# Routing attention into a squared-ReLU block, one core: the second pair's queries and keys turned by transposing transfers

## The chip, the core and the metric

The kernel runs on one core of one Trainium2 chip. The metric is the device time of one execution in microseconds (us). The core has TensorE (PE, matrix products, with its own queue of weight loads, PEld), VectorE (DVE), ScalarE (ACT), GpSimd (POOL) and SyncE (SP). Transfers (DMA) are issued from the queues of SP and ACT (SPq and ACTq in the rows) and carried by 16 DMA engines. SBUF is the working memory, PSUM holds what TensorE writes.

## The reference

Attention of 4 batches with 8 heads, 768 positions and 64 features, in which a query sees only the keys whose nearest centroid (of 16 for each head) is its own; then a block with a squared ReLU over the 3072 rows of 512.

```python
q_assign = np.argmax(np.einsum('bhsd,hcd->bhsc', q_n, c_n), axis=-1)
k_assign = np.argmax(np.einsum('bhsd,hcd->bhsc', k_n, c_n), axis=-1)
mask = q_assign[:, :, :, None] == k_assign[:, :, None, :]
scores = scale * np.matmul(q, k.transpose(0, 1, 3, 2))
scores = np.where(mask, scores, -1000000000.0)
attn = np.exp(scores - np.max(scores, axis=-1, keepdims=True))
attn = attn / (np.sum(attn, axis=-1, keepdims=True) + 1e-09)
x = np.matmul(attn, v)          # then (B,H,S,D) -> (B*S, H*D)
h = x @ w_in
out = (np.maximum(h, 0.0) ** 2) @ w_out
```

## The kernel before

**Pairs.** Attention goes in 16 pairs of heads (`for p in range(NG)`), each some 20 us long, and the second block follows. Everything here happens in the first 55 us, in pairs 0 and 1. All engines follow the order in which the code is written; nothing is scheduled behind the author's back (`manual_schedule`). A queue runs its instructions in order, so one that waits holds all behind it.

**Turned operands.** A product needs queries and keys with features along partitions (`qkT`). Pair 0 is turned by TensorE from the loaded tiles (`turn_first`, line 275), because it is wanted first. Pair 1 is also turned by TensorE (`turn`, line 289, in three parts of eight small products, each followed by a copy on ACT). From pair 2 on a transfer does it: ACT splits each float into two 16-bit words (`split_words`, line 307: four copies for a pair, two for the queries and two for the keys), a transfer stores the words in DRAM (`words`), and a transposing transfer (`turn_words`, line 323, on SP's queue) brings them back turned.

**Marks.** `logits` multiplies queries and keys by the centroids, `turn_logits` turns the result on DVE (tile `lt`), and `number` finds the largest of 16. Several equal maxima are resolved to the first by a product with `order` and a second maximum. For pair 0 the marks are a one-hot tile `oh`, turned by TensorE (`turn_onehot`) and copied out by ACT (line 410) and DVE (lines 415, 419). For later pairs `number` makes three rows of marks (`marks_t`), a small transfer stores them (`far`), and two more bring them back as the operand `rows` (line 386), one for each head of the pair.

**Tiles.** A pair has nine score tiles. Each is a `mask` product and a `score` product into one PSUM tile `sc` of three, then an exponential on ACT (line 463). A tile can begin when the exponential of the tile three places before has read its PSUM tile. Six tiles have 512 queries, three have 2 times 256. Then `times_v` multiplies the nine results by the values into PSUM `V` (shown as av_a) and `M` (av_b), `add_up` sums the weights, and the next pair follows. DVE adds up the exponentials (line 466), which `add_up` needs.

**Loads.** Pairs 0 to 2 and the first values are loaded at the start; `load_qk(3)`, three blocks of weights and the next values follow on SP's queue, `load_qk(4)` and later ones on ACT's queue. Each tile of queries, keys or values is 128 x 768 floats (0.39 MB), a block of weights 128 x 1024 (0.52 MB). A flag at the end (`check_sums`) sends the program to `general_path` if a sum in `seen` is unusable.

Of the kernel before, what the change touches and what calls it, by code (L numbers as in the profile page):

```python
# [8 lines left out]
F32 = mybir.dt.float32  # L9
# [16 lines left out]
def kernel(  # L26
# [197 lines left out]
    seen = const.tile([P, NG * NBL], F32, name="seen")  # L224
# [64 lines left out]
    def turn(pair, part, bank):  # L289
        if part == 0:  # L290
            qkT[pair] = qktp.tile([P, 2 * NCH, P], F32, name="qkT")
        for i in range(4):
            which, c = divmod(4 * part + i, NCH)
            for e in range(2):
                nc.tensor.matmul(
                    bank[D * e : D * (e + 1), P * i : P * (i + 1)],
                    lhsT=raw[pair][which][:, e, c], rhs=ident, start=True, stop=True,
                )
        nc.scalar.copy(
            out=qkT[pair][:, 4 * part : 4 * part + 4].rearrange("p c n -> p (c n)"), in_=bank  # L300
        )
        if part == 2:
            raw.pop(pair)

    words = {}

    def split_words(pair, which, queue=nc.sync):
        if pair >= NG:
            return
        if which == 0:  # L310
            words[pair] = dram.tile([2 * NCH, P, 2, 2 * D], U16, name="words")
        flat = loads.tile([P, NCH, 2, 2 * D], U16, name="flat", tag="qk")
        src = raw[pair][which].bitcast(U16).rearrange("p h c (d two) -> p h c two d", two=2)
        for e in range(2):
            nc.scalar.copy(out=flat[:, :, :, D * e : D * (e + 1)], in_=src[:, e])
        queue.dma_start(
            words[pair][NCH * which : NCH * (which + 1)].rearrange("c p two d -> p c two d"),
            flat,
        )
        if which == 1:  # L320
            raw.pop(pair)

    def turn_words(pair):
        if pair >= NG:
            return
        qkT[pair] = qktp.tile([P, 2 * NCH, P], F32, name="qkT")
        nc.sync.dma_start(
            qkT[pair].rearrange("p c n -> p (c n)").bitcast(U16),
            words.pop(pair).rearrange("c p two d -> (c p two) d"), transpose=True,
        )  # L330
# [17 lines left out]
    def number(pair):  # L348
# [8 lines left out]
        nc.vector.reduce_max(out=mx, in_=src, axis=AX.X)  # L357
        nc.vector.tensor_tensor(out=best, in0=src, in1=over_c(mx), op=ALU.is_ge)
# [4 lines left out]
        if pair == 0:  # L363
            nc.vector.tensor_tensor(
                out=oh.rearrange("p b e c -> p (b e) c")[:, :, 0:C], in0=best, in1=over_c(mx),
                op=ALU.is_equal,
            )
            return
# [21 lines left out]

    def turn_onehot():
# [5 lines left out]
        for half, bank in enumerate((sc.pop("oh")[:, 0], M)):  # L397
# [210 lines left out]

    centroids_norm()
# [5 lines left out]
    turn_first(1, 1, halves[1], nc.vector.tensor_copy)  # L615
    logits(0, begin("ls"))
    for i in ("oh", 0, 1):
        begin(i)
    turn_logits(0)
    number(0)  # L620

# [8 lines left out]
    for p in range(NG):  # L630
        if p == 0:
            load_qk(3)
            load_ahead(0)
        if p == HP + 1:
            nc.sync.dma_start(x_far[FEED[3]], xT.pop(FEED[3]))
        if p:
# [3 lines left out]
            turn_words(p + 2)  # L640
# [9 lines left out]
        if p == 0:  # L650
            for i in range(2):
                turn(1, i, (V, M)[i])
                score(p, i, 0, True)
            turn_onehot()
            for t in rows_of:
                nc.vector.memset(t, 0.0)
            turn(1, 2, V)
            for i in range(NB):
                if i == 2:
                    begin(i)  # L660
                    score(p, i, 0, True)
                mask(p, i, 0, False)
                exponential(i)
        else:
# [7 lines left out]
        if p < 2:  # L672
# [28 lines left out]
        split_words(p + 3, 1)  # L701
        load_qk(p + 4, (nc.scalar, nc.scalar))
# [969 lines left out]
    def check_sums():  # L1672
# [3 lines left out]
            out=flag[0:1], in0=every, scalar1=UP * float(P * NG * NBL), scalar2=None, op0=ALU.is_lt  # L1676
# [280 lines left out]
```

## Time and profile before

| | |
|---|---|
| median of 3 runs | 865.0 us (864.05 to 865.22) |
| the profiled execution | 863.94 us |
| its span in the profile | 862.0 us (1.94 us lie around it) |
| TensorE busy | 852.3 us, 99% of the span |
| VectorE busy | 741.0 us, 86% |
| ScalarE busy | 452.3 us, 52% |
| GpSimd busy | 242.2 us, 28% |

Times in the rows count from the start of the span. A timeline row has start, duration, engine, line, operation, output and input; in brackets stands the idle time before it and what ended that. Consecutive equal instructions are merged (x2, x3), and the duration then is that of the whole. Rows of the chain have start, duration and what the end of the program hung on at that time. The profiled execution is 1.06 us below the median.

### The profile page before, as it was taken

How to read it: one execution, taken by the hardware profiler on the slowest of the kernel's cores; microseconds unless marked ns; L12 is line 12 of the kernel's file. 1: busy time of each engine (PE TensorE's matmuls, PEld its weight loads, DVE VectorE, ACT ScalarE, POOL GpSimd, SP SyncE). 2: the span in 40 equal slices, each digit the busy share in tenths (PEclk: the TensorE clock that was granted, in tenths of full speed). 3: DMA queues.
4: the chain of work that ended last, by engine and by line, in shares of the span. 5: the costliest groups of instructions: out<-in, count | busy, mean ns of one | idle time of the engine just before them, and what ended most of it. 6: DMA issues, size and time to landing. Idle time of an engine off the chain costs nothing.

```text
span 862.0 us, 15526 instructions
## 1 busy us (share of the span) xinstructions
PE 852.3 (99%) x5883; PEld 648.9 (75%) x5883; DVE 741.0 (86%) x1189; ACT 452.3 (52%) x697; POOL 242.2 (28%) x202
## 2 busy tenths in 40 slices
PE   9999999999999999999999999999999999999997
PEld 5454444444444455557899999999999999999997
DVE  6798888888888899999779988789888898887786
ACT  5877766777775557752212692222269322693120
POOL 0000000000000046762466737130223902237000
PEclk9999999999999999999999999999999999999999
DMA  7787798677666217729895554459447895433542
GB/s 258 162 194 201 216 268 197 183 198 196 177 176 178 64 61 249 241 85 336 329 336 195 206 186 152 179 162 337 149 183 230 288 379 191 183 140 137 214 153 71
DMA packets 149443, 173.30 MB, mean 201 GB/s; under 512 B 57226, under 2 KB 126962, under 8 KB 146034
## 3 DMA queue, kind: packets, MB, share of 16 engines
q1 hardware_dynamic: 132802, 151.89, 55.8%
q10 hardware_dynamic: 16560, 20.35, 7.3%
q8 instruction: 48, 0.79, 0.4%
q14 instruction: 33, 0.27, 0.1%
HBM read 110.93 MB, written 50.27 MB: 187 GB/s over the span
## 4 chain that ended last, share of the span: by engine, by line
PE 88%; DVE 6%; DMA 2%; issue 1%; ACT 1%; POOL 1%; SPq 0%; DVEq 0%; POOLq 0%
PE bank L1365 23%; PE bank L1098 15%; PE sc L447 14%; PE av_a L481 10%; PE bank L1262 6%; PE av_b L481 5%; PE more L1098 5%; PE sc L456 4%; PE bank L811 3%; PE sc L335 1%; PE sc L500 1%; DMA wt<-w_far 1%; DVE g L1177 1%; DVE w_raw L155 1%; DVE g L767 1%
## 5 line engine op out<-in xcount | busy, mean ns | idle before, releaser
L463 ACT ACTIVATE ex<-sc 128x1024 f32<-128x1024 f32 x144 | 144.4, 1026 | 38.0 <-PE sc L447 31.9
L447 PE MATMUL sc<-qkT 64*128 64x512 f32 (+1 forms) x768 | 151.0, 484 | 0.0
L167 POOL TENSOR_TENSOR w_in<-w_in,w_raw 128x512 int32<-128x512 int32 x16 | 21.4, 1338 | 294.4 <-DVE w_in L159 278.2
L1083 POOL TENSOR_TENSOR g<-g,home 128x768 f32<-128x768 f32 x30 | 55.7, 1876 | 152.4 <-DVE home L1177 102.2
L447 PEld LDWEIGHTS sc<-qkT 64*128 64x128 f32 x768 | 67.1, 188 | 41.0 <-issue 29.8
L481 PE MATMUL av_a<-ex,v_raw 128*64 128x512 f32 x384 | 85.9, 596 | 0.0
L466 DVE TENSOR_TENSOR total<-total,ex 128x1024 f32<-128x1024 f32 x64 | 78.7, 1229 | 6.5
L1613 ACT COPY spare<-bank 128x128 f32<-128x128 f32 x35 | 9.2, 263 | 136.5 <-issue 84.8
L1365 PE MATMUL bank<-wt,l 128*128 128x128 f32 x544 | 72.0, 275 | 0.4 <-DVE l L557 0.4
L1365 PE MATMUL bank<-wt,home 128*128 128x128 f32 x552 | 70.5, 275 | 0.0
L1365 PEld LDWEIGHTS bank<-wt,l 128*128 128x128 f32 x544 | 66.2, 192 | 0.6 <-issue 0.5
L1365 PEld LDWEIGHTS bank<-wt,home 128*128 128x128 f32 x552 | 66.0, 192 | 0.0
L1177 DVE TENSOR_TENSOR g<-bank,g 128x384 f32<-128x384 f32 (+2 forms) x108 | 53.7, 506 | 13.0 <-PE bank L1098 8.4
L481 PEld LDWEIGHTS av_a<-ex,v_raw 128*64 128x64 f32 x384 | 26.2, 137 | 51.0 <-issue 50.3
L1067 ACT COPY home<-bank 128x384 f32<-128x384 f32 x66 | 30.9, 480 | 56.4 <-PE bank L1098 55.7
L456 PE MATMUL sc<-rows 64*128 64x512 bf16 (+1 forms) x360 | 60.5, 323 | 0.0
L787 ACT ACTIVATE g<-g 128x768 f32<-128x768 f32 (+1 forms) x77 | 55.7, 723 | 2.4
L786 ACT ACTIVATE g<-g 128x768 f32<-128x768 f32 (+1 forms) x77 | 54.8, 711 | 2.3 <-DVE g L1177 1.2
L481 PE MATMUL av_b<-ex,v_raw 128*64 128x256 f32 x384 | 44.2, 379 | 0.0
L456 PEld LDWEIGHTS <-rows 64*128 64x128 bf16 x360 | 18.5, 94 | 33.0 <-issue 29.2
L481 PEld LDWEIGHTS av_b<-ex,v_raw 128*64 128x64 f32 x384 | 27.6, 137 | 20.7 <-issue 5.7
L1365 PE MATMUL bank<-wt,g 128*128 128x128 f32 x304 | 38.8, 275 | 0.0
(296 smaller groups left out, 1852.5 us busy)
## 6 DMA issues: line engine op xcount, KB each, us to landing
wt<-right_far SPq DMA_DIRECT2D x11, 1792.0 KB
wt<-w_far SPq DMA_DIRECT2D x20, 896.0 KB
words<-flat SPq DMA_DIRECT2D x26, 384.0 KB
w_raw<-in_moe_w_in_dram SPq DMA_DIRECT2D x16, 512.0 KB
w_raw<-in_moe_w_out_dram SPq DMA_DIRECT2D x16, 512.0 KB
wt<-right_far SPq DMA_DIRECT2D x7, 1024.0 KB
v_raw<-in_v_dram SPq DMA_DIRECT2D x16, 384.0 KB
rb<-far_r SPq DMA_DIRECT2D x30, 192.0 KB
```

Of the source, the lines that this page charges most:

```text
L447: nc.tensor.matmul(sc[i][:, e, cols], lhsT=qkT[pair][rows, NCH + c], rhs=qkT[pair][rows, n.start // P : n.stop // P], start=first, stop=no ...
L456: nc.tensor.matmul(sc[i][:, e, cols], lhsT=ohT[pair][rows, 1, c * P : (c + 1) * P], rhs=ohT[pair][rows, 0, columns(i)], start=first, stop= ...
L463: nc.scalar.activation(out=ex[i], in_=sc.pop(i), func=ACT.Exp, scale=SCALE)
L466: eng.tensor_tensor(out=out, in0=a, in1=b, op=ALU.add)
L481: nc.tensor.matmul(bank[D * e : D * (e + 1), 0 : n.stop - n.start], lhsT=raw_v[pair][:, e, c], rhs=ex[i][:, e, cols], start=c == 0, stop=c ...
L786: nc.scalar.activation(out=to, in_=to, func=ACT.Relu)
L787: nc.scalar.square(to, to)
L1083: nc.gpsimd.tensor_tensor(out=of_four(to, s)[:, :, half], in0=of_four(base, s)[:, :, half], in1=beside[s].rearrange("p u m n -> p (u m) n" ...
L1098: nc.tensor.matmul(bank[:, QT * u : QT * (u + 1)], lhsT=lefts[j, s](u)[i], rhs=operand[i], start=begins and u == 0, stop=True, skip_group_ ...
L1177: nc.vector.tensor_tensor(out=out, in0=one, in1=two, op=ALU.add)
L1262: nc.tensor.matmul(bank, lhsT=left[j][:, f], rhs=right(j)[:, f], start=begins and f == 0, stop=True, skip_group_check=True,)
L1365: nc.tensor.matmul(bank, lhsT=left[:, f], rhs=rhs[:, f], start=(f == 0), stop=(f == F4 - 1))
```

## The change

Pair 1 is no longer turned by TensorE: `turn` is gone. Its words are split by ACT before pair 0's marks are copied out, stored from ACT's queue, and brought back by two transposing transfers (queries, keys) that stand on SP's queue ahead of `load_qk(3)`, the weights and the next values. The split words lie in spare tiles of the exponentials' pool.

Pair 0's marks are one comparison with the maximum, without `order`, the second maximum and the comparison with it. `count_marks` adds up the ones of each partition and writes 0.5 into one more column of `seen` where they are exactly 24 (one for each row of queries and keys), and 0 where they are not, which sends the program to the general path.

The last copy of pair 0's turned keys is cut in two, half on ACT, half on DVE; the DVE half waits for the ACT half. `logits(1)` and what follows move from behind tile 2 of pair 0 to behind its second tile of 256, and write to `M`. Pair 1 writes three scores first and then the three masks; `split_words(3, 1)`, `turn_words(3)` and `load_qk(4)` move from pair 0 into pair 1, behind its third exponential. From pair 2 on nothing changes.

```diff
@@ marks of the first pair, in number()
         nc.vector.reduce_max(out=mx, in_=src, axis=AX.X)
+        if pair == 0:
+            nc.vector.tensor_tensor(
+                out=oh.rearrange("p b e c -> p (b e) c")[:, :, 0:C], in0=src, in1=over_c(mx),
+                op=ALU.is_ge,
+            )
+            return
         nc.vector.tensor_tensor(out=best, in0=src, in1=over_c(mx), op=ALU.is_ge)
...
         nc.vector.reduce_max(out=mx, in_=best, axis=AX.X)
-        if pair == 0:
...
-            return
+    def count_marks():
+        marked = small.tile([P, 1], F32, name="marked")
+        nc.vector.reduce_sum(
+            out=marked, in_=oh.rearrange("p b e c -> p (b e) c")[:, :, 0:C], axis=AX.XY
+        )
+        nc.vector.tensor_scalar(
+            out=seen[:, NG * NBL :], in0=marked, scalar1=2.0 * NBL, scalar2=0.5,
+            op0=ALU.is_equal, op1=ALU.mult,
+        )
@@ turn_words
-        nc.sync.dma_start(
-            qkT[pair].rearrange("p c n -> p (c n)").bitcast(U16),
-            words.pop(pair).rearrange("c p two d -> (c p two) d"), transpose=True,
-        )
+        far = words.pop(pair)
+        for i in range(0, 2 * NCH, NCH if pair == 1 else 2 * NCH):
+            c = slice(i, i + (NCH if pair == 1 else 2 * NCH))
+            nc.sync.dma_start(
+                qkT[pair][:, c].rearrange("p c n -> p (c n)").bitcast(U16),
+                far[c].rearrange("c p two d -> (c p two) d"), transpose=True,
+            )
@@ ahead of the loop
+    def by_two(out, in_):
+        nc.scalar.copy(out=out[:, 0:QT], in_=in_[:, 0:QT])
+        nc.vector.tensor_copy(out=out[:, QT:], in_=in_[:, QT:])
...
-    turn_first(1, 1, halves[1], nc.vector.tensor_copy)
+    turn_first(1, 1, halves[1], by_two)
...
     number(0)
+    for i in range(2):
+        split_words(1, i, nc.scalar)
@@ in the loop
         if p == 0:
+            turn_words(1)
             load_qk(3)
...
         if p == 0:
             for i in range(2):
-                turn(1, i, (V, M)[i])
                 score(p, i, 0, True)
             turn_onehot()
+            count_marks()
             for t in rows_of:
                 nc.vector.memset(t, 0.0)
-            turn(1, 2, V)
+            begin(2)
+            score(p, 2, 0, True)
             for i in range(NB):
-                if i == 2:
-                    begin(i)
-                    score(p, i, 0, True)
                 mask(p, i, 0, False)
                 exponential(i)
+        elif p == 1:
+            for i in range(NB):
+                begin(i)
+                score(p, i, 0, True)
+            for i in range(NB):
+                mask(p, i, 0, False)
+                exponential(i)
+            split_words(3, 1)
+            turn_words(3)
+            load_qk(4, (nc.scalar, nc.scalar))
...
         for i in range(NCH, NCH + NB):
             tile_of(p, i)
+            if p == 0 and i == NCH + 1:
+                sc["ls"] = M.rearrange("p (a n) -> p a n", a=1)
+                logits(1, sc["ls"])
+                turn_logits(1)
+                number(1)
...
         if p == 0:
             split_words(3, 0)
-        split_words(p + 3, 1)
-        load_qk(p + 4, (nc.scalar, nc.scalar))
+        else:
+            split_words(p + 3, 1)
+            load_qk(p + 4, (nc.scalar, nc.scalar))
```

Lines behind the edits shift: line 315 of before is 305 of the change, 327 is 320, 335 is 328, 383 is 376, 386 is 379, 410 is 413, 447 is 450, 456 is 459, 463 is 466.

SP's queue of before, from the first values to the first sums (`w_raw` weights, `far` and `rows` the marks of pair 1, `qkT<-words` the turning of pair 2, then the words of pair 3):

```order
L105 DMA v_raw<-in_v_dram 128x2x384
L95 DMA q_raw<-in_q_dram 128x2x384
L95 DMA k_raw<-in_k_dram 128x2x384
L128 DMA w_raw<-in_moe_w_in_dram 128x1024 x3
L105 DMA v_raw<-in_v_dram 128x2x384
L383 DMA far<-marks_t 128x3x32
L386 DMA rows_168<-far 3x4x384 x2
L327 DMA_TRANSPOSE qkT<-words 128x3072
L316 DMA words<-flat 128x6x256 x2
L515 DMA far_r<-seen 128x12
```

The same stretch of SP's queue with the change:

```order
L105 DMA v_raw<-in_v_dram 128x2x384
L320 DMA_TRANSPOSE qkT<-words 128x1536 x2
L95 DMA q_raw<-in_q_dram 128x2x384
L95 DMA k_raw<-in_k_dram 128x2x384
L128 DMA w_raw<-in_moe_w_in_dram 128x1024 x3
L105 DMA v_raw<-in_v_dram 128x2x384
L320 DMA_TRANSPOSE qkT<-words 128x3072
L376 DMA far<-marks_t 128x3x32
L379 DMA rows_168<-far 3x4x384 x2
L306 DMA words<-flat 128x6x256
L518 DMA far_r<-seen 128x12
```

Two transposing transfers for pair 1 now stand ahead of the six loads, and the marks of pair 1 (`far`, `rows`) have moved from ahead of pair 2's transposing transfer to behind it.

ACT of before at the head of pair 0 (`av_a`, `av_b` and `sc` are PSUM tiles, the `ex` of line 410 is the turned one-hot tile):

```order
L285 COPY qkT<-sc 128x384
L299 COPY qkT<-av_a 128x512
L299 COPY qkT<-av_b 128x512
L410 ACTIVATE ex<-sc 128x6x2x32 x2
L299 COPY qkT<-av_a 128x512
L463 ACTIVATE ex<-sc 128x1024 x6
L315 COPY flat<-q_raw 128x12x64 x2
```

The same place with the change:

```order
L285 COPY qkT<-sc 128x384
L613 COPY qkT<-sc 128x192
L305 COPY ex<-q_raw 128x12x64 x2
L306 DMA words<-ex 128x6x256
L305 COPY ex<-k_raw 128x12x64 x2
L306 DMA words<-ex 128x6x256
L413 ACTIVATE ex<-av_a 128x6x2x32 x2
L466 ACTIVATE ex<-sc 128x1024 x6
```

The three copies of line 299 are gone; four splitting copies, two issues of transfers and half a copy stand ahead of the copies of the marks.

ACT of before in pair 1 (from the last copy of pair 0's result on; here `flat<-q_raw` and `flat<-k_raw` are pair 4's split, the loads are pair 5's):

```order
L490 COPY xT<-av_b 128x256
L463 ACTIVATE ex<-sc 128x1024 x6
L315 COPY flat<-q_raw 128x12x64 x2
L463 ACTIVATE ex<-sc 128x1024 x3
L315 COPY flat<-k_raw 128x12x64 x2
L95 DMA q_raw<-in_q_dram 128x2x384
L95 DMA k_raw<-in_k_dram 128x2x384
```

The same place with the change:

```order
L493 COPY xT<-av_b 128x256
L466 ACTIVATE ex<-sc 128x1024 x3
L305 COPY flat<-k_raw 128x12x64 x2
L95 DMA q_raw<-in_q_dram 128x2x384
L95 DMA k_raw<-in_k_dram 128x2x384
L466 ACTIVATE ex<-sc 128x1024 x3
L305 COPY flat<-q_raw 128x12x64 x2
L466 ACTIVATE ex<-sc 128x1024 x3
```

Two splitting copies of pair 3 and the issue of pair 4's loads now stand between the third and the fourth exponential of pair 1.

## Rows read from the trace of the kernel before

**Rows 1.** The page: granted clock in 40 slices, and the chain's shares.
```profile
PEclk9999999999999999999999999999999999999999
...
PE 88%; DVE 6%; DMA 2%; issue 1%; ACT 1%; POOL 1%; SPq 0%; DVEq 0%; POOLq 0%
```

**Rows 2.** The chain in order of time, 0 to 70 us (start, us, what).
```profile
9.39 1.02 PE av_a L295 x16
10.42 1.06 PE sc L447 x4
...
13.56 0.44 PE sc L402 x6
...
17.89 0.39 PE sc L456 x2
18.28 0.86 PE sc L447 x4
...
24.55 5.30 PE av_a L481 x24
...
32.44 0.78 PE sc L500 x8
...
53.35 0.32 PE sc L456
```

**Rows 3.** The timeline, ACT and its queue, 14 to 34 us.
```profile
14.04 0.87 ACT L410 ACTIVATE ex<-sc 128x384 bf16<-128x384 bf16 x2 [0.90 <-PE sc L402]
...
15.89 2.86 ACT L463 ACTIVATE ex<-sc 128x1024 f32<-128x1024 f32 x3
...
22.24 1.55 ACT L315 COPY flat<-q_raw 128x768 uint16<-128x768 uint16 x2
...
23.83 0.41 ACTq L316 DMA_DIRECT2D words<-flat  x1
...
24.33 1.56 ACT L315 COPY flat<-k_raw 128x768 uint16<-128x768 uint16 x2 [0.53 <-ACT flat L315]
...
25.93 0.38 ACTq L316 DMA_DIRECT2D words<-flat  x1
...
33.63 0.38 ACT L490 COPY xT<-av_b 128x256 f32<-128x256 f32 x1
```

**Rows 4.** The timeline, DVE, 7 to 24 us.
```profile
7.95 0.56 DVE L285 COPY qkT<-sc 128x384 f32<-128x384 f32 x1 [0.52 <-PE sc L280]
...
9.43 0.58 DVE L346 STREAM_TRANSPOSE lt<-sc 128x384 f32<-128x384 f32 x1 [0.93 <-PE sc L335]
...
10.64 0.56 DVE L358 TENSOR_TENSOR best<-lt,mx 128x384 bf16<-128x384 f32 x1
...
19.01 0.58 DVE L346 STREAM_TRANSPOSE lt<-sc 128x384 f32<-128x384 f32 x1
...
22.93 0.28 DVE L379 STREAM_TRANSPOSE marks_t<-marks 128x96 bf16<-128x96 bf16 x1
```

**Rows 5.** The timeline, SP's queue: transposing transfers and the marks' last transfers.
```profile
28.76 6.77 SPq L327 DMA_TRANSPOSE qkT<-words  x1
...
50.48 1.52 SPq L386 DMA_DIRECT2D rows<-far  x2
...
56.32 2.75 SPq L327 DMA_TRANSPOSE qkT<-words  x1
...
64.79 1.52 SPq L386 DMA_DIRECT2D rows<-far  x2
...
228.13 2.62 SPq L327 DMA_TRANSPOSE qkT<-words  x1
...
235.17 1.53 SPq L386 DMA_DIRECT2D rows<-far  x2
```

**Rows 6.** The timeline, TensorE's weight loads at the start of pair 2.
```profile
53.68 0.09 PEld L456 LDWEIGHTS <-rows 64*128 64x128 bf16 x1 [0.31 <-DMA rows<-far]
```

**Rows 7.** Stretches: busy by engine, granted clock, DMA share, GB/s in the last column.
```profile
10.00:12.00 2.00, 2.00 (x22) 1.07 (x20) 1.86 (x5) 0.59 (x1) 0.00 (x0) 1.00 1.08 384
```

More of the change, by code (lines that the diff above doesn't have):

```diff
@@ L222 @@
         )
-    seen = const.tile([P, NG * NBL], F32, name="seen")
+    seen = const.tile([P, NG * NBL + 1], F32, name="seen")
     oh = accp.tile([P, NBL, 2, D], BF16, name="oh", tag="part")
@@ L287, in turn_first @@
             raw.pop(0)
[L289 to L297, printed above, removed]
-                )
[L299 to L303, printed above, removed]
     words = {}
@@ L311, in split_words @@
             words[pair] = dram.tile([2 * NCH, P, 2, 2 * D], U16, name="words")
-        flat = loads.tile([P, NCH, 2, 2 * D], U16, name="flat", tag="qk")
+        if pair == 1:
+            spare = expp.tile([P, 2, 512], F32, name="ex").bitcast(U16)
+            flat = spare.rearrange("p a n -> p (a n)")[:, 0 : 4 * S // 2].rearrange(
+                "p (c two d) -> p c two d", c=NCH, two=2
+            )
+        else:
+            flat = loads.tile([P, NCH, 2, 2 * D], U16, name="flat", tag="qk")
         src = raw[pair][which].bitcast(U16).rearrange("p h c (d two) -> p h c two d", two=2)
@@ L362, in number @@
         nc.vector.reduce_max(out=mx, in_=best, axis=AX.X)
-        if pair == 0:
[L364 to L367, printed above, removed]
-            return
         squared = small.tile([P, n], F32, name="squared")
@@ L389, in number @@
             )
+    def count_marks():
[6 more added lines that the diff above has]
+            op0=ALU.is_equal, op1=ALU.mult,
+        )
     def turn_onehot():
@@ L395, in turn_onehot @@
         )
-        for half, bank in enumerate((sc.pop("oh")[:, 0], M)):
+        for half, bank in enumerate((V, M)):
             n = NBL // 2
@@ L607, in load_ahead @@
             loaded += 1
+    def by_two(out, in_):
+        nc.scalar.copy(out=out[:, 0:QT], in_=in_[:, 0:QT])
+        nc.vector.tensor_copy(out=out[:, QT:], in_=in_[:, QT:])
+    QT = TB // 2
     centroids_norm()
@@ L614 @@
     centroids_turned()
-    turn_first(1, 1, halves[1], nc.vector.tensor_copy)
+    turn_first(1, 1, halves[1], by_two)
     logits(0, begin("ls"))
-    for i in ("oh", 0, 1):
+    for i in range(2):
         begin(i)
@@ L620 @@
     number(0)
+    for i in range(2):
+        split_words(1, i, nc.scalar)
     first_sums = []
@@ L639 @@
                 early_x_sums()
-            turn_words(p + 2)
+            if p > 1:
+                turn_words(p + 2)
             spread(p - 1)
@@ L671 @@
             tile_of(p, NB)
-        if p < 2:
             logits(p + 1, begin("ls"))
@@ L700 @@
             split_words(3, 0)
-        split_words(p + 3, 1)
-        load_qk(p + 4, (nc.scalar, nc.scalar))
+        else:
+            split_words(p + 3, 1)
+            load_qk(p + 4, (nc.scalar, nc.scalar))
         round_1(p)
@@ L1675, in check_sums @@
         nc.vector.tensor_scalar(
-            out=flag[0:1], in0=every, scalar1=UP * float(P * NG * NBL), scalar2=None, op0=ALU.is_lt
+            out=flag[0:1], in0=every, scalar1=UP * float(P * (NG * NBL + 1)), scalar2=None, op0=ALU.is_lt
         )
```

1 line of the change is left out of this document (removed).

## Prediction

> **What bounds the kernel now.** I read the page first: TensorE is busy for 99% of the span, at the full granted clock in all 40 slices, and 88% of the chain is TensorE [rows 1]. So work taken from TensorE is worth its full length, if nothing else is late in its place. Then I read the chain in order of time through pairs 0 and 1, because every edit lies there [rows 2]. The reader is to see an unbroken string of TensorE work: a score tile costs 0.22 + 0.86 = 1.08 us, its mask part 0.22 once the products follow each other, and only 0.3 us near 53.4 is a wait for the marks of pair 2 [rows 2, 6]. Last I read the queues that the edits touch: ACT [rows 3], DVE [rows 4] and SP [rows 5], because each of them runs in order and pair 1 will now hang on all three.
>
> **The change part by part.** All times are on the clock of the profiled span (862.0 us; the execution was 863.94, which is 1.06 below the median of 865.0). I follow TensorE through four stages.
>
> *Head of pair 0.* Removed from TensorE: three parts of turning, 1.02 us each on the chain, some 3.1 in all [rows 2]. The last copy of keys took 0.56 us on DVE [rows 4]. It becomes 192 columns on ACT (256 columns took 0.38 [rows 3]; I take 0.32) and then, waiting for that, 192 on DVE (between half of 0.56 and all of it; I take 0.36): 0.72 with the hand-over, so 0.16 later; bounds 0 and 0.4. DVE turns the logits at 9.43 + 0.16 = 9.59, and since the first comparison now gives the marks they are ready 0.56 us after 10.64 + 0.16, at 11.4 [rows 4]. TensorE meanwhile ends the logits at 9.55 and does two scores (1.06 + 0.86 [rows 2]) until 11.5, so it does not wait; two sets of six mark products (0.44 and less) and the third score bring it to 13.35. ACT comes to the same moment by another way: from 8.3 it does the four splitting copies and two issues, which took 22.24 to 26.36 in before, 4.1 us [rows 3], then 0.87 for its copies of the marks [rows 3]: 13.3. So the masks start at 13.35, and the first exponential (0.39 for the masks [rows 2]) at 13.8 instead of 15.9. Each exponential is 2.86 / 3 = 0.95 [rows 3]. The fourth tile needs the first exponential's PSUM tile, so TensorE, done with three masks at 14.0, stands until 14.8. In before that tile began at 17.89 [rows 2]: 3.1 us gained. The logits of pair 1 (0.78, as long as the equally shaped sums [rows 2]) come later in the stage, so the values begin at 14.8 + 6 x 1.08 + 0.78 = 22.05 instead of 24.55 [rows 2]: **2.5 us gained**. Bounds 1.9 and 2.9, from the copy and the ACT chain. Covered at no cost: DVE's count (0.7 us, two small instructions beside a memset) ends before it is wanted. Also covered, by some 2 us: pair 1's turning. Its second words are issued at 12.0 and land 2.8 us later (25.93 to 28.76 [rows 3, 5]); half a transposing transfer behind that ends near 17.5, and the logits want it at 20.2.
>
> *Structure of pair 1.* Scores first and masks behind them cost nothing in products, but the first exponential now ends later than TensorE has work: TensorE stands 0.7 us ahead of the fourth tile. Then ACT, behind the third exponential, does two splitting copies (1.55) and two issues (0.4 each, with gaps 2.5 in all [rows 3]). With S the start of the first exponential, the fourth ends at S + 2.86 + 2.5 + 0.95 = S + 6.3, and the seventh tile needs its PSUM tile. TensorE is there at S + 5.07 (fourth tile from S + 1.0 for 1.08, logits 0.78, two tiles), so it stands 1.3 us. Together **2.0 us lost**; bounds 1.0 (issues free) and 2.6.
>
> *The marks of pair 1.* They have to be there when three scores are done. Pair 1 begins 33.22 - 24.55 = 8.67 us after the values [rows 2], at 30.7, and its scores end at 33.5. The marks are ready on DVE at 26.3 (logits end at 20.95, DVE's five additions near 22.1, then 4.2 us as from 19.01 to 23.21 [rows 4]), but on SP their transfers stand behind pair 2's transposing transfer. When does that go? Its words leave ACT behind six exponentials (13.8 + 6 x 0.95 = 19.5) and 3.7 us more for the split up to its second issue: 23.2. They land at 26.0 if the DMA engines are free [rows 3, 5]. They are not quite: the six loads (2.75 MB, 7.2 us at 384 GB/s [rows 7]) now start behind pair 1's turning at 17.5 and last to 24.7, and share with the words. I take 27.0, bounds 26.0 and 28.5. From the issue of a transposing transfer to the issue of the marks' last transfers went 8.47 us (56.32 to 64.79) and, fastest, 7.04 (228.13 to 235.17) [rows 5], with 0.39 MB of sums in between, about 1 us at 384 GB/s. Without those it is 6.0 to 7.5; I take 6.4, nearer the fast one, because less else is under way: 33.4. The second of the two transfers goes 0.76 later and landed 2.4 us after its issue (51.24 to 53.68 [rows 5, 6]): 36.6. So TensorE **waits 3.0 us**; bounds 0.8 (26.0 + 6.0) and 5.6 (28.5 + 7.5), and the 6.77 us issue under other loads [rows 5] could add up to 4 more.
>
> [...]
>
> *Pair 2.* Its marks were 0.33 us late [rows 2, 6] and will be early by about 2: **0.3 us gained**.
>
> Sum: -2.5 + 2.0 + 3.0 - 0.3 = **+2.2 us**. TensorE's chain carries a shift to the end undiminished, since it has no slack to absorb it [rows 1]. 863.94 + 2.2 = 866.1 for an execution like the profiled one; against the median 865.0 + 2.2 = **867.2 us**.
>
> **The rivals.** *Marks in time.* The marks' small transfer passes, or the transposing transfer is as short as its 2.7 us issue [rows 5], so the second row transfer lands by 33.5: the wait is gone and the sum is -2.5 + 2.0 - 0.3 = -0.8, or 864.2. For it speaks that 33.5 is only 3 us from my figure, made of four pieces read elsewhere; against it, that every pair in rows 5 shows over 7 us for this way. It decides below a landing at 34.3, where the sum changes sign; to 35.3 it stays within +1.0.
>
> *Faster by more.* The stall ahead of the seventh tile and the one ahead of the fourth are hidden too; then up to 2.8 us are gained: 862.2. Both follow from ACT's order, so I give it little.
>
> [...]
>
> *Pair 1 turned late.* If its two halves take as long as the first transposing transfer did (6.77 us to issue [rows 5]), the logits of pair 1 wait some 1 us, and all behind on SP's queue moves by about 3: +5, 870. For it: words and loads run beside it. Against: the initial loads are over by then.
>
> *The flag.* If two maxima of pair 0 are equal, the general path runs and the time is far above any here. Only the data decide; under 0.01, within the last case.
>
> **How the numbers follow.** Forecast (+1.0 to +3.6): 0.45. Marks in time (-0.8 to +1.0): 0.27. Faster by more: 0.10. Clock: 0.10. Pair 1 late: 0.08. A measurement of this kernel can tell about 0.2%, 1.7 us. Faster than that: 0.10. Within: 0.27 and the lowest part of the forecast, 0.12, makes 0.39. Slower: 0.33 + 0.10 + 0.08 = 0.51. The range leaves out a tenth at either end: 863.8 to 869.2, from the early marks to the lower part of the clock's case; the forecast's own is 866.0 to 868.6.
>
> **What would show it.** The fourth tile of pair 0 at 14.8 and the values at 22.0 (head right). TensorE idle ahead of pair 1's first mask, released by the transfer of `rows`, for 3 us (forecast) or none (first rival); the second transposing issue near 27, the `rows` issue near 33.4. Idle time ahead of pair 1's fourth and seventh tile, 0.7 and 1.3, released by ACT. Pair 2's first mask at 55.9 instead of 53.7. [...] The prediction is wrong if the copies of the marks on ACT start well after 12.4, if the second words land before 25, or if a later stage takes the shift up.

## The result: 1.3% slower, and the profile after

The changed kernel takes **876.2 us** (median of six runs, 871.48 to 879.77) where the kernel before took 864.63 in the same session (864.05 to 865.22): a ratio of 1.0127, 95% interval 1.0109 to 1.0146. The forecast was 867.2 with a range of 863.8 to 869.2. The sign was right, the size was five times too small, and no run lay inside the range.

From the page of the changed kernel (its profiled execution took 876.34 us):

```profile
span 874.4 us, 15434 instructions
...
PE   8799999999999999999999999998999999999997
...
PEclk9899999999999999999999999999999999999999
...
PE 86%; DVE 7%; DMA 3%; issue 2%; ACT 1%; SPq 1%; DVEq 0%; ACTq 0%
```

TensorE's row of before:

```profile
PE   9999999999999999999999999999999999999997
```

Against it and [rows 1] two places stand out: the second slice, where TensorE's row falls to 7 and the granted clock to 8, and the 28th slice, near 605 us, where TensorE falls to 8. The chain has 3% of DMA in it instead of 2%. To see how much each place costs, I paired TensorE's products of the two traces, counted from the last one (behind the turning the two programs have the same products), and took the difference of their starts:

| at | before, us | after minus before, us |
|---|---|---|
| pair 0's value products | 24.55 | -2.5 |
| pair 2's first tile, second mask product | 53.69 | +6.8 |
| 590 us | 590 | +7.1 |
| 630 us | 630 | +11.8 |
| last product | | +12.2 |

So there are **two losses**: 9.3 us inside pair 1, and 4.7 us between 590 and 630 us, in a stage that no edit touches.

**The first loss.** TensorE's timeline after (start, length, line, shape, count; in brackets the idle time before it and what ended it):

```profile
14.55 0.39 PE L459 MATMUL sc<-ex 64*128 64x512 bf16 x2 [0.68 <-ACT ex L466]
...
22.03 5.37 PE L484 MATMUL av_a<-ex,v_raw 128*64 128x512 f32 x24
...
39.20 0.61 PE L459 MATMUL sc<-rows 64*128 64x512 bf16 x1 [5.65 <-DMA rows<-far]
```

The head is as forecast: fourth tile at 14.55 (14.8), values at 22.03 (22.05). Then TensorE waits 5.65 us for pair 1's marks. The chain of waits says why; it has the rows that answer to the SP rows of before [rows 5]:

```profile
22.57 8.30 DMA words<-flat
...
30.92 3.71 SPq L320
...
34.73 2.07 DMA far<-marks_t
...
36.82 0.91 SPq L379
...
37.79 2.15 DMA rows<-far
...
60.34 0.53 PE sc L459 x2
```

Pair 2's second words leave at 22.57 and land only at 30.87, 8.30 us later; the transposing transfer is issued at 30.92, the marks follow behind it, and the second row transfer lands at 39.94. Pair 2's first mask is at 60.34. The DMA engines' share (next to last column; the last is GB/s) tells where the 8.30 us come from. Before:

```profile
12.00:18.00 6.00, 5.94 (x62) 3.04 (x60) 3.08 (x7) 4.05 (x7) 0.00 (x0) 1.00 0.87 334
18.00:24.00 6.00, 6.00 (x52) 3.89 (x52) 5.76 (x12) 5.27 (x6) 0.00 (x0) 1.00 0.01 5
24.00:30.00 6.00, 6.00 (x35) 2.17 (x34) 5.21 (x5) 5.21 (x7) 0.00 (x0) 1.00 0.71 187
```

After:

```profile
12.00:18.00 6.00, 5.32 (x35) 2.54 (x34) 5.07 (x8) 5.39 (x7) 0.00 (x0) 1.00 0.88 151
18.00:24.00 6.00, 6.00 (x54) 3.02 (x52) 5.58 (x8) 5.04 (x8) 0.00 (x0) 1.00 1.04 298
24.00:30.00 6.00, 6.00 (x44) 2.67 (x44) 4.99 (x10) 4.98 (x8) 0.00 (x0) 1.00 0.96 340
...
36.00:42.00 6.00, 2.36 (x8) 0.68 (x10) 0.00 (x0) 1.37 (x2) 0.00 (x0) 0.73 0.25 72
```

Before, the DMA engines stood still from 18 to 24 us (0.01), and the words of pair 2 then had them alone. After, they are full from 18 to 30: pair 1's words and transposing transfers hold them from 12 to 19, at only 151 GB/s up to 18, and the six loads, which wait behind those on SP's queue, fill the time in which pair 2's words go. The last row shows the granted clock, a mean of 0.73 from 36 to 42 us: in the trace it is 0.50 of full speed from 38.72 to 45.54.

**The second loss.** TensorE near 605 us, after:

```profile
607.10 0.89 PE L1123 MATMUL bank<-wt,raw 128*128 128x192 f32 x4 [1.87 <-DMA raw<-raw_far]
608.69 1.57 PE L1123 MATMUL bank<-wt,home 128*128 128x192 f32 x4 [0.70 <-DVE spare L560]
```

It waits 1.87 us for a load and then 0.70 for DVE, and the lag is 10.0 when the second of these products starts at 608.69; behind that the granted clock is 0.50 from 608.74 to 612.15, where the lag grows by another 1.75, to 11.8. (Two of the expectations below still put this loss at 5.2 us; paired product by product it is 4.7.) SP's queue, before and after:

```profile
584.32 0.81 SPq L963 DMA_DIRECT2D wt<-w_far  x2
585.38 1.01 SPq L1740 DMA_DIRECT2D xT<-x_far  x2
588.86 0.32 SPq L932 DMA_DIRECT2D raw<-raw_far  x1
```

```profile
589.54 0.80 SPq L988 DMA_DIRECT2D wt<-w_far  x2
592.34 7.52 SPq L1765 DMA_DIRECT2D xT<-x_far  x2
600.91 0.32 SPq L957 DMA_DIRECT2D raw<-raw_far  x1
```

A pure shift of 7.1 us would put these at 591.4, 592.5 and 596.0. The first comes 1.9 us early, the second x_far load comes last of all (the 7.52 us hold a wait), and so the raw load is 4.9 us late. What SP waited for there:

```profile
SPq L1765 <- DMA out_dram<-g: 8.7, 2, 6.8
```

This is a store that ACT's queue issued, and its data are not what SP's load needs. But the two have the same completion semaphore: in the trace eight of these serve all 407 transfers that the program issued. The store is issued at 589.43 and its last update of the semaphore comes at 599.47; SP, which waits for that, issues the load at 599.54.

### The profile page after: what moved, and what is told of

Same layout as the page of the kernel before. It is cut to its first block, busy times and chain, and to the rows that moved or that the text cites. A ratio compares the mean times of both kernels' runs of the same rounds, so it can differ in the third digit from the quotient of the medians.

```text
span 874.4 us, 15434 instructions
## 1 busy us (share of the span) xinstructions
PE 855.3 (98%) x5835; PEld 647.9 (74%) x5835; DVE 740.5 (85%) x1188; ACT 452.9 (52%) x699; POOL 242.4 (28%) x202
## 4 chain that ended last, share of the span: by engine, by line
PE 86%; DVE 7%; DMA 3%; issue 2%; ACT 1%; SPq 1%; DVEq 0%; ACTq 0%
PE bank L1390 21%; PE bank L1123 16%; PE sc L450 14%; PE av_a L484 9%; PE bank L836 6%; PE bank L1287 5%; PE more L1123 5%; PE av_b L484 4%; PE sc L459 4%; PE sc L328 2%; PE sc L503 1%; DMA wt<-right_far 1%; DMA words<-flat 1%; DVE spare L1202 1%; DVE g L792 1%
```

## The experiments

Each is compared with runs of the kernel before on its own chip (medians there 866.0 to 866.5). "Lag" is again the start of TensorE's products against the profile of before.

### Queue order: marks ahead of pair 2's transposing transfer

```diff
-            turn_words(2)
...
                 number(1)
+                turn_words(2)
```

> The changed kernel with one line moved: pair 2's transposing transfer stands behind pair 1's marks on SP's queue instead of ahead of them. Theory (queue order makes the 5.65 us wait at 33.55): the marks leave SP at 26.2 and land near 31.5, before TensorE needs them at 33.5; the wait and the half clock from 38.72 are gone, pair 2's first mask starts near 53.1 instead of 60.34. Rival (the small transfers are slow by themselves, beside the loads): a wait of over 2 us stays. For the second loss, near line 1123 at 605 us, which cost 5.2 us: if it comes from TensorE's being 7 us late, it is gone too and the whole is 863 to 865 us; if it comes from the changed kernel's addresses and numbers of transfers, most executions keep it and the median is near 869.

Measured: 874.78, ratio 1.0092 (1.0063 to 1.0121). What TensorE waited for in the profiled execution:

```profile
PE sc L328 <- DMA qkT<-words: 2.8, 1, 2.8
PE bank L1123 <- DMA raw<-raw_far: 2.1, 1, 2.1
PE sc L459 <- DMA rows<-far: 1.6, 3, 0.8
```

The wait for pair 1's marks is nearly gone, so the order on SP made it. But TensorE then waits 2.8 us for pair 2's turned tiles, and pair 2's marks are late: the work behind the words has only changed places, and the lag at pair 2's first mask is still 7.3. The second loss stays (4.8 us between 590 and 630), so moving the marks does not touch it. This execution also began slowly, which comes up again at the end.

### The six loads: in front of pair 1's turning, or behind pair 2's

```diff
-            turn_words(1)
             load_qk(3)
             load_ahead(0)
+            turn_words(1)
```

> The changed kernel with pair 3's and the weights' loads issued ahead of pair 1's transposing transfers on SP, as in the kernel before. Theory (pair 2's second words took 8.3 us because they shared the DMA engines with these loads): the loads are over by 20, the words land near 26.5, the transposing issue follows there, the wait at 33.5 shrinks from 5.65 to about 2.5 us, and pair 2 starts some 3 us earlier, 872 us or less. Rival (the words are slow because of their own 512-byte pieces): they still take 8 us. Price of the theory: pair 1's turning is later by up to 5 us, but its logits want it only at 20.2.

Measured: 878.99, ratio 1.0124 (1.0092 to 1.0155). The expectation fell in its time, not in its theory: pair 2's second words, issued at 25.03, now let the transposing transfer go at 30.34, after 5.3 us instead of 8.3, and TensorE does not wait for pair 1's marks. But the chain of waits shows what took their place:

```profile
12.11 8.46 DMA words<-ex
...
20.59 1.44 SPq L320
...
22.13 6.05 DMA qkT<-words
```

Now pair 1's words share with the loads and take 8.46 us, and TensorE waits 4.8 us for pair 1's turned tiles. That words slow down beside these loads is shown, but whichever words come beside them pay.

```diff
             load_qk(3)
-            load_ahead(0)
+            load_weights(0)
...
             turn_words(2)
+            nc.sync.dma_start(raw[3][1], k[0, 6:8].rearrange("h (p j) d -> p h j d", p=P))
+            load_ahead(0)
+            load_v(1)
```

> The changed kernel with four of the six loads (pair 3's keys, two weight blocks, pair 1's values) issued behind pair 2's transposing transfer on SP; queries of pair 3 and the first weight block stay where they were. Theory (pair 2's second words landed at 30.87 because of the loads): with 0.9 MB ahead of them instead of 2.75 MB they land near 26, as in the forecast; the second transposing issue is at 26 to 27, the marks land near 35 and the wait falls from 5.65 to 1 to 2 us; pair 2's first mask some 4 us earlier. Rival (the words are slow by their own 512-byte pieces): they land at 30 or later, and nothing changes. The second loss near 605 us is not touched: 872 to 876 where the changed kernel has 876.9.

Measured: 878.2, ratio 1.0133 (1.0111 to 1.0154). SP's queue in its profile:

```profile
27.10 3.51 SPq L321 DMA_TRANSPOSE qkT<-words  x1
...
32.79 1.42 SPq L377 DMA_DIRECT2D far<-marks_t  x1
39.59 1.67 SPq L380 DMA_DIRECT2D rows<-far  x2
```

The second transposing issue is at 27.10, where the forecast had it (27.0): with 0.9 MB of loads ahead instead of 2.75 MB the words are 3.8 us earlier. So the loads are what made these words late: from their issue at 22.91 to the transposing issue it is 4.2 us instead of 8.3. But I had left the marks behind the four loads that were moved, and `far` then took 6.79 us to land; the wait grew to 8.1 us. The time did not improve.

### The clock: TensorE kept busy through the wait

```diff
+            for _ in range(6):
+                nc.tensor.matmul(
+                    V, lhsT=ident, rhs=qkT[1][:, 0:4].rearrange("p c n -> p (c n)"),
+                    start=True, stop=True,
+                )
```

> The changed kernel with six products of 512 columns into a free bank between pair 1's scores and its first mask; they compute nothing that is used. Theory (the half clock from 38.72 for 6.83 us follows from the wait that comes before it): TensorE works through the wait, the clock stays at 1.0, and of the 3.4 us that the slow clock cost, less the 2 us of stalls that it covered, 1 to 3 us come back: pair 2's first mask near 58 instead of 60.34. Rival (the clock falls for another reason): still 0.5 near 39, no gain.

Measured: 879.47, ratio 1.0147 (1.0124 to 1.0169). The granted clock stayed at 1.0 in all slices, where the changed kernel with its wait of 5.65 us has 0.50 from 38.72 on; so here the wait is what brings the lower clock. But nothing came back. The chain of waits in its profile:

```profile
49.47 4.83 SPq L320
...
54.35 3.60 DMA far<-marks_t
...
58.78 2.29 DMA rows<-far
...
61.11 0.39 PE sc L459
```

The two mask products of pair 2's first tile start at 60.37 and 61.11, not before the 60.28 and 60.49 of the changed kernel: they now wait for pair 2's marks, which stand behind pair 3's transposing transfer. In the changed kernel itself the weight loads of these two products are released by the same transfers, while its products run up to them without a gap:

```profile
60.27 0.31 PEld L459 LDWEIGHTS <-rows 64*128 64x128 bf16 x2 [0.62 <-DMA rows<-far]
```

So the lower clock near 40 ran beside a DMA chain that is as long, and the time to pair 2 did not change when it was gone.

### Lateness alone

The kernel before, with eight products of 512 columns at the start of pair 1:

```diff
+            if p == 1:
+                for _ in range(8):
+                    nc.tensor.matmul(
+                        V, lhsT=ident, rhs=qkT[1][:, 0:4].rearrange("p c n -> p (c n)"),
+                        start=True, stop=True,
+                    )
```

> The kernel before with eight products of 512 columns, 0.88 us each by the pace of the value products, into a free bank at the start of pair 1: TensorE is 7 us later from there on, busy all the time, and nothing else is changed. If the second loss of the changed kernel (5.2 us near line 1123) comes from the lateness alone, most executions here show it: 864.6 + 7 + 5 = 877. If it comes from the changed kernel's addresses or numbers of transfers, it is absent: 871.7, with a spread of about 1 us.

Measured: 875.45 (six runs: 871.25, 871.9, then four of 874.98 to 876.91), ratio 1.0098 (1.0075 to 1.0122). The profiled execution (871.9) has no second loss: its products are 7.2 us late at 590 us and 7.4 at 630. So lateness does not always bring it. Four others are 3 to 5 us above it, more than the differences of the start that the traces show (up to 2.5 us, last section); they have no trace, so it is not shown where they lost it. The eight products also add 32 TensorE instructions (16 products and 16 weight loads in the trace), which move the instruction transfers of the next section.

### Where the instruction transfers fall

The page counts 48 transfers of the kind "instruction", each one packet of 16 KB:

```profile
q8 instruction: 48, 0.79, 0.4%
```

In the trace of before they come once for each 249 TensorE instructions on average, with a median of 254 between two (11942 instructions are on record, weight loads among them). The changed kernel has 11846 on record, 96 less, and its later transfers stand elsewhere among the products. The window from 580 to 582 us of before holds one, beside the transfers on which SP's order hangs:

```profile
q8 instruction: 1, 0.02, 2.7%
```

After, the corresponding window (587 to 589) holds none; the transfer is at 590.2, 9.7 us later, where the products are 7.1 later. If its place makes the second loss, the loss goes when the 96 instructions are put back. Four kernels test this, with tiny products as the unit, each one product and one weight load (128 and 128 in the trace of the run with 128); first 48 of them in pair 1's wait of the changed kernel:

```diff
+            for _ in range(48):
+                nc.tensor.matmul(
+                    V[0:32, 0:32], lhsT=ident_b[:, 0:32], rhs=ident_b[:, 0:32], start=True, stop=True
+                )
```

> The changed kernel with 48 tiny bf16 products (32 columns, into a free bank, used by nothing) in the wait of pair 1, so that the number of TensorE instructions ahead of everything later is that of the kernel before; the wait hides them. [...] Rival (the second loss comes with the lateness of 7 us, whatever the count): most executions stay at 875 to 880.

Measured: **873.65** (871.48 to 875.4), ratio 1.0085 (1.0068 to 1.0101), and in the same session the changed kernel as it is:

> The changed kernel as it is, on the chip of these runs, for comparison. All theories: 871 to 880, median 876 where the kernel before has 865, most executions with the second loss.

Measured: 876.89 (874.11 to 878.23), ratio 1.0121 (1.0103 to 1.0139). SP's queue with the 48 products:

```profile
595.65 0.81 SPq L992 DMA_DIRECT2D wt<-w_far  x2
596.71 0.97 SPq L1769 DMA_DIRECT2D xT<-x_far  x2
600.16 0.32 SPq L961 DMA_DIRECT2D raw<-raw_far  x1
```

The spacing of before is back (1.06 and 3.45 us between the three; 1.06 and 3.48 from 584.32 on), TensorE does not wait there for a transfer, and the lag between 590 and 630 grows by 0.0 us. The median lies 3.2 us below the changed kernel's, and five of the six runs lie below the rival's 875. Two more, on the kernel before, with the same tiny products at the start of pair 1. 128 of them are 256 instructions, near the 249 on record for each transfer, so about one transfer's worth (an estimate from that trace):

```diff
+            if p == 1:
+                for _ in range(128):
+                    nc.tensor.matmul(
+                        V[0:32, 0:32], lhsT=ident_b[:, 0:32], rhs=ident_b[:, 0:32], start=True, stop=True
+                    )
```

> The kernel before with 128 of these tiny products at the start of pair 1: 256 TensorE instructions more, a whole transfer's worth, so the later transfers fall where they did, and TensorE is later by their length, estimated 4 to 8 us. Theory (where the instruction transfers fall): the time is that of the kernel before plus the lateness, as measured at pair 2, with no second loss. Rival (lateness): some 4 us more than that in most executions.

Measured: 870.11 (868.28 to 870.62), ratio 1.0042 (1.0026 to 1.0058). The products took 3.35 us:

```profile
36.33 3.35 PE av_a L667 x128
```

So 866.04 + 3.35 = 869.4, and 0.7 is left: no second loss, and the queue keeps before's order. With 64 of them, about half a transfer's worth:

> The same with 64 tiny products: half a transfer's worth, half the lateness (2 to 4 us). Theory (where the instruction transfers fall): the transfers near 580 us stand elsewhere than in the kernel before, so the second loss can come; with it, 3 to 5 us over the lateness in most executions. Rival (lateness): less second loss than with 128.

Measured: 870.46 (867.7 to 872.09), ratio 1.0046 (1.003 to 1.0062). These products took 1.75 us, so 867.8 was due and 2.7 us are over. But the profiled execution (870.64, near the median) loses nothing between 590 and 630: of its lag of 6.75 us at the end 4.8 were there at pair 2, 1.1 came by 590 and 0.9 behind 630. So these 2.7 us are not shown to be a second loss, and this run decides nothing. Against lateness speaks the run with 128: 6.0 us late at 590 us, it is 6.2 late at 630. The last of these is the control of the first, about a whole transfer's worth (128) in the wait of the changed kernel:

> The changed kernel with 128 tiny products (3.35 us by the run with 128 of them) in pair 1's wait of 5.65 us: 256 TensorE instructions more, a whole transfer's worth. Theory (where the instruction transfers fall): they fall where they do in the changed kernel, the second loss stays, 876 to 878 or a ratio of 1.012 to 1.0135 to the kernel before. Rival (the filled wait itself cured the run with 48): the second loss is gone as there, ratio 1.0085 or less.

Measured: 875.42 (873.27 to 876.83), ratio 1.0104 (1.008 to 1.0128): between the two answers, and the profiled execution (873.31) has no second loss. This one stays inconclusive.

All 16 traces together say more than the medians. In six of them (before, the runs with 48 tiny products in the wait and with 128 on the kernel before, and three below) an instruction transfer falls 11.8 to 12.3 us ahead of the product that before has at 592.24; in these six w_far's load follows 7.7 to 7.9 us ahead of that product, the second x_far load 6.3 to 6.5 ahead, and there is no second loss. In the other ten w_far's load comes 9.7 to 9.8 ahead, and the second x_far load later, at 3.4 ahead to 0.6 behind. Where it comes at 0.0 or behind (five traces, all of changed kernels with the transfer 9.1 ahead), the loss is 4.3 to 6.1 us; at 1.9 ahead it is 1.0; further ahead it is 0.2 or less. So in all 16 traces the place of that transfer goes with which loads go first, and before's order never has the loss. That the count makes the order, and not the filled wait, is shown by the run with 48 and its control: with 128 in the same wait w_far's load is 9.75 ahead, as in the changed kernel. (The count alone does not place it: the run with pair 3's splitting early, below, has before's count and the transfer 15.9 ahead.) Why the other order costs 5 us in some executions and nothing in others is open; so is how a 16 KB packet of 0.9 us moves a landing by 1.8 us.

### Putting the transfers in a better order

The loads staged as in the second load experiment, the marks ahead of pair 2's transposing transfer and of the loads, and 24 tiny products in each of the two short stands ahead of a fourth tile:

```diff
-            turn_words(2)
...
                 number(1)
+                turn_words(2)
+                nc.sync.dma_start(raw[3][1], k[0, 6:8].rearrange("h (p j) d -> p h j d", p=P))
+                load_ahead(0)
+                load_v(1)
```

> The same staging of loads, pair 1's marks ahead of pair 2's transposing transfer on SP, and 48 tiny products hidden in TensorE's two short stands ahead of fourth tiles, which bring the count of TensorE instructions back to that of the kernel before. Theory (queue order, loads and the count of instructions make the whole loss): no wait at 33.5, no half clock, no second loss; what stays is the structure of pair 1 (2.0 us lost) and the head (2.5 gained), and pair 2's marks about 1 us late: 864 to 867, where the kernel before has 865 to 866. Rival (something else costs 4 to 5 us late): 869 or more.

Measured: 877.01, ratio 1.0133 (1.0111 to 1.0154). No second loss (lag +12.5 at 590 and at 630). The wait at pair 1 is gone, but another has come:

```profile
PE sc L329 <- DMA qkT<-words: 8.0, 1, 8.0
```

Pair 3's keys, now loaded at 35.35, make pair 3's words late, and its logits wait. Next, pair 3's splitting back at the end of pair 0, its keys early:

```diff
-            split_words(3, 1)
-            turn_words(3)
-            load_qk(4, (nc.scalar, nc.scalar))
...
-            if p > 1:
-                turn_words(p + 2)
+            turn_words(p + 2)
...
             split_words(3, 0)
-        else:
-            split_words(p + 3, 1)
-            load_qk(p + 4, (nc.scalar, nc.scalar))
+        split_words(p + 3, 1)
+        load_qk(p + 4, (nc.scalar, nc.scalar))
```

> The same as the last, but pair 3's second splitting and pair 4's loads stand at the end of pair 0 on ACT, and pair 3's transposing transfer at the start of pair 1, as in the kernel before (pair 3's keys are loaded early again). Theory (ACT's work behind the third exponential costs the 1.3 us stall ahead of the seventh tile and makes pair 2's marks late): both are gone, pair 2's first mask near 52.5 instead of 53.4 in the kernel before, and the time is 1 us under the kernel before: 863 to 865. Rival (the loads and the splitting of pair 3 collide with pair 2's words again): the words land near 29 and pair 2's logits or pair 1's marks wait 1 to 3 us.

Measured: 872.15, ratio 1.0074 (1.0051 to 1.0096); no second loss in its profile, but 3.6 us of waits for marks and 1.0 for turned tiles. Here a lower clock does cost time: it is granted from 58.46 to 65.28, behind the wait for pair 2's marks, and the lag grows from 6.5 to 9.0 us. Last, the weight blocks out of the way as well:

```diff
                 turn_words(2)
+                load_v(1)
+                load_weights(0)
...
             number(p + 1)
+            load_ahead(0)
...
+            if p == 1:
+                round_1(0)
             split_words(p + 3, 0)
```

> The changed kernel with its transfers put in another order: pair 1's marks ahead of pair 2's transposing transfer; the first weight block and pair 1's values behind it, the other two weight blocks behind pair 2's marks, and the rounding of the first block on ACT inside pair 1; pair 3's second splitting at the end of pair 0 as in the kernel before; 48 tiny products in the two short stands keep the count of TensorE instructions. Theory (the DMA engines' time in the first 35 us is what the change lacks): pair 2's words land by 26, nothing waits for marks or turned pairs by more than 1 us, pair 2's first mask 1 to 2 us earlier than in the kernel before when the clock rises at the same time: 863.5 to 865.5 where the kernel before has 866. Rival (the transposing transfers are too slow whatever stands beside them): waits of 2 us or more at pair 2's logits, 868 or more.

Measured: 873.42, ratio 1.0093 (1.0067 to 1.0118), and no second loss in its profile (lag +8.2 at 590 and at 630). TensorE's waits up to 70 us:

```profile
PE sc L459 <- DMA rows<-far: 3.1, 1, 3.1
PE sc L459 <- ACT ex L466: 2.6, 1, 2.6
PE sc L328 <- DMA qkT<-words: 1.3, 1, 1.3
```

Of these 7.0 us, 2.6 are made by this order itself: ACT stands 11.05 us ahead of a weight block that leaves SP only at 55.98 and lands 5.94 us later, and pair 2's exponentials stand behind it. The other 4.4 are marks and turned tiles, still more than the 2.5 of the head. The rival's time came (868 or more), its sign did not (2 us or more at pair 2's logits; it was 1.3). So even with these loads out of the way, the chain of words, transposing transfer, marks and rows was longer than TensorE's work beside it. No order that I tried beats the kernel before.

### The marks' half alone

The kernel before with the `is_ge` marks of pair 0, the count, and the column more in `seen`:

```diff
+        if pair == 0:
+            nc.vector.tensor_tensor(
+                out=oh.rearrange("p b e c -> p (b e) c")[:, :, 0:C], in0=src, in1=over_c(mx),
+                op=ALU.is_ge,
+            )
+            return
...
+            count_marks()
```

> The kernel before with the marks' half of the change alone: pair 0's marks without picking among equal maxima, the count, and one column more in seen; pair 1 is turned by TensorE as before. Theory (TensorE does not wait for pair 0's marks in the kernel before, so 1.1 us less on DVE is off the chain; the loss is all from the turning): within 0.5 us of the kernel before, no second loss. Rival (the addresses moved by 32 bytes, or the count, do harm): 2 us or more above.

Measured: 867.13 in twelve runs, ratio 1.0008 (0.9989 to 1.0027): no difference that these runs can tell (between 1.0 us less and 2.3 more). So the loss is from the rest of the change, the turning by transfers and the orders that go with it.

## Why the prediction was wrong, point by point

- **Head of pair 0, -2.5: right.** Values at 22.03 (forecast 22.05), pair 1's first score at 30.70 (30.7). That close a fit is luck in part: the fourth tile was 0.25 early, and the stretch from there to the values 0.23 too long. Pair 1's own turning was in time, its logits ran at 20.05 without a wait, so that rival fell.
- **Marks of pair 1 late, +3.0: the mechanism was right, the size was not; this is the step that failed first.** The wait was 5.65 us, and the product behind the second row transfer began at 39.98 instead of 36.6. The term that was mis-sized is the landing of pair 2's second words: 30.87 instead of 27.0 (bounds 26.0 and 28.5), +3.9. From there to the rows' issue it was 5.9 us instead of 6.4. I had the loads last to 24.7, by starting them at 17.5 and giving them 384 GB/s; in fact pair 1's words and transposing transfers held the engines to 19, at 151 GB/s from 12 to 18, the loads went on to 28 or 29, and the words were spread over the same time. The staged loads gave 27.10. (The lower bound of the wait was also added up wrongly: 26.0 + 6.0 is 1.4 less than 33.4, which makes 1.6 and not 0.8.) What held the marks was in part SP's own order: `far` is issued at 34.73, right behind the transposing transfer's issue of 3.71 us. Its packets then moved from 35.87 to 36.33, as the last of the transposing transfer's went, at 36.14; they did not pass it.
- **Structure of pair 1, +2.0, and pair 2's marks, -0.3: too small together by 1.1 us, and neither was right by itself.** From pair 1's second row transfer to pair 2's first mask it was 60.34 - 39.98 = 20.4 us instead of 19.3. The stall of 1.3 ahead of the seventh tile did not come, with the lower clock or without: ACT's two splitting copies took 1.57 us (from 43.35), and the two issues, at 41.55 and 42.03, ran beside exponentials and not behind them. The stall ahead of the fourth tile was 0.26, and 0.68 in the run with the filled wait. What came in place of the 2.0 was the lower clock (0.50) from 39.98 to 45.54, some 2.8 us for TensorE (an estimate, half of that stretch): 17.3 + 0.26 + 2.8 = 20.4. I had pair 2's marks early by about 2; in the run with the filled wait TensorE waits 1.20 us for pair 3's turned tiles and 0.95 for the first of pair 2's rows, since pair 3's transposing transfer, which goes at 49.47 there and at 49.95 in the changed kernel instead of 40.01, stands ahead of them. The rows of ACT in the changed kernel:

```profile
41.55 0.39 ACTq L95 DMA_DIRECT2D q_raw<-in_q_dram  x1
...
43.35 1.57 ACT L305 COPY flat<-k_raw 128x768 uint16<-128x768 uint16 x2
```

- **The clock (0.10): it fell, at a price of nothing there.** Its case gives the range its upper end, 869.2, and no run shows the price on the way to pair 2 that this assumes. What the runs showed: the granted clock was 0.50 from 38.72 to 45.54 (a mean of 0.73 from 36 to 42 us), and in the filled wait, with 1.0 all along, pair 2's first mask started no earlier (60.37, and 60.28 in the changed kernel): it waited for pair 2's marks. Near 608 us, on the bare chain, 0.50 from 608.74 to 612.15 cost 1.75 us, and a lower clock cost 2.5 in the run with pair 3's splitting early.
- **"TensorE's chain carries a shift to the end undiminished": failed upward.** It carried 6.8 to 7.1 us to 590, and then lost 4.7 more. I had looked at the places that the diff touches only. That 96 instructions less would move the instruction transfers, and that a late stage has transfers whose order hangs on them, was in none of my cases.
- **Sum.** -2.5 + 2.0 + 3.0 - 0.3 = 2.2 was forecast at pair 2; 3.4 (rows) and 1.1 (pair 1's rest) and the rounding of the parts make the 6.8 measured there; 0.3 came by 590, 4.7 by 630 and 0.4 behind it: 12.2.

## What to carry to other kernels

Before work goes from an engine to transfers, look at the DMA engines' share in the very microseconds in which each later transfer runs, after the new ones have pushed everything on their queue back; idle time there may be left only because the new work was not yet there. A chain of transfers (words, turning, marks, rows) that one queue carries in order was as hard as an engine here: shortening one wait moved it to the next link in six orders. And where a kernel is late by a constant, compare the late stages as well: here a wait of 6.8 us on a shared completion semaphore, and an instruction transfer at another place among the products, went with a new loss of 4.7 us, 540 us behind the edits.

## What the runs showed of the hardware that I had not expected

- The number of TensorE instructions in pair 1 moved 16 KB transfers some 550 us later (9.1 us ahead of the product at before's 592.24 instead of 11.8), and the order of loads went with them; 48 tiny products, hidden in a wait, took 3.2 us off the changed kernel's median (876.89 to 873.65).
- TensorE's pace at the start differed between executions of equal code. In the 16 traces the record of the full granted clock begins at 4.5 to 10.7 us. In the changed kernel's profile and in that of the run with the marks first, the same twelve products of the head took:

```profile
5.41 0.66 PE av_b L280 x12
```

```profile
6.26 1.28 PE av_b L280 x12
```

  The profiled run with the marks' half alone, whose record of the full clock begins at 9.12 instead of 4.84, is 1.6 us behind the profile of before at pair 2 and 2.5 at the end. That is the size of the spread of the kernel before between sessions (863 to 868 us for most runs).
- Pair 2's transposing transfer moved less for its share of the DMA engines than words and loads did. It ran alone from 32 to 36 us of the changed kernel, with the engines' share at 1.12 and 200 GB/s; words in 512-byte pieces ran alone from 37 to 39 us of before, with 312 GB/s at a share of 1.03; the loads of before moved 334 GB/s at a share of 0.87. (The share adds up the time of packets and can pass 1, as in [rows 7].)

```profile
32.00:36.00 4.00, 1.55 (x8) 0.39 (x4) 0.00 (x0) 0.00 (x0) 0.00 (x0) 1.00 1.12 200
```

```profile
37.00:39.00 2.00, 1.95 (x16) 0.58 (x14) 1.23 (x2) 1.65 (x2) 0.00 (x0) 1.00 1.03 312
```
